# A new order list and another first fill for a planned attention and feed-forward kernel

## The chip, the cores and the metric

The kernel runs on one core of one Trainium2 chip. The metric is the device time of one execution in microseconds (us), the median of several runs. The core has five engines that matter here: TensorE (PE in the profile; its weight loads are PEld), VectorE (DVE), ScalarE (ACT), GpSimd (POOL), and SyncE (SP), which here only issues DMA transfers. Each engine runs its own instructions in their order and waits on semaphores for the others.

## The reference

Inputs `q`, `k`, `v` have 8 batches, 8 heads, 576 positions and a head size of 64, all float32. Attention works in chunks: the 576 positions are 9 chunks of 64, and each chunk looks only at itself.

```python
scores = scale * np.matmul(q_c, k_c.transpose(0, 1, 2, 4, 3))     # per chunk of 64
attn = softmax(scores); out = np.matmul(attn, v_c)
x = out.transpose(0, 2, 1, 3).reshape(B, S, 512)
h = np.maximum(x @ w_in, 0.0)                                      # 512 -> 1024
conv = sum(conv_w[k] * h shifted by k - 1 positions for k in 0, 1, 2)
y = (h * sigmoid(conv)) @ w_out                                    # 1024 -> 512
```

The result is 8 x 576 x 512 in float32. The convolution's neighbours are rows of the same batch; beyond its ends stand zeros.

## The kernel before

**Tiles, units and pairs.** The 4608 rows (batch and position) are cut in three ways. Attention works on 36 tiles of 128 rows (t0 to t35, two chunks each). The first matrix and the convolution work on 12 units of about 384 rows (u0 to u11) times 8 slices of 128 columns of `w_in`, so 96 blocks; a step such as `mm1(1,5)` is unit 1, slice 5. The second matrix works on 18 pairs of tiles (256 rows).

**Precision.** TensorE's fast format is rounded float32 (`float32r`), so each operand is split in a high and a low part (`x_h`, `x_l`, `wi_h`, `wi_l`, `wo_h`, `wo_l`), and each product is three: high times high, high times low, low times high. The `w_in` and `w_out` products therefore take 12 matmuls a block. `w_out` is used with seven products for a pair instead of eight, which need sums and differences of the weights' quarters and of the gated rows (`w_diff`, `f_sum`).

**From load to output.** A tile's q and k are loaded (`load_rows`, in three slots for tiles 0 to 8), transposed on TensorE (`t_pe`, line 198), and copied to SBUF (`t_copy`). `scores` is on TensorE (line 250), the softmax on VectorE and ScalarE (`s_max` to `s_rec`), its division on GpSimd or VectorE (`s_norm`, line 322), its transpose on TensorE again (`p_pe`, line 329), then `attn_v` (line 342). `x_hi` and `x_lo` (line 401) split the result. `mm1` (line 411) multiplies by `w_in`; `h_relu` (line 419 or 421), `c_mid`, `c_left`, `c_right` (line 454), `c_sig` and `c_mul` (line 484) make the gated rows. `f_hi` (lines 77 and 79), `f_lo` (line 502) and `f_sum` (line 505) prepare a pair's factors, `product` (line 515) multiplies by `w_out`, and `o_copy`, `o_both` (line 533) and `o_last` gather the seven products. From tile 9 on, q and k come by way of a copy in device memory and are transposed on VectorE (`t_dve`, line 220), from tile 12 on two tiles share a softmax (`both` on TensorE, `s_fold`, line 306, `s_scale`, line 310, `p_dve`).

**Weights.** They arrive as 64-bit numbers in two w slots, and are turned into float32 by `w_scale` (ScalarE, line 561), `w_shift` (VectorE) and `w_words` (VectorE, line 570), whose end frees the slot. Then come the splits: `w_hi` and `w_left` for `w_in`; for each of four parts of `w_out`: `w_hi_q`, `w_diff` (GpSimd, lines 592 to 594), `w_lo_q` (line 587), `w_hi_d` (line 77) and `w_lo_d` (line 600). All of `w_out` must be ready before the first `product`. Steps 57 to 65 are its last part: 57 the load, 60 `w_words`, 61 `w_hi_q`, 62 `w_diff`, 63 `w_lo_q`, 64 `w_hi_d`, 65 `w_lo_d`.

**What sets the order.** The function doesn't emit instructions as it goes. Each piece of work is a `step()` with an engine, the steps that it must follow, and in `other` the engines that could do it as well; there are 1,873. A list `moved_` gives some steps another engine (an entry is 4 times the step's number plus which of the others). A list `order_` then names all 1,873 steps in the order in which a plan places them: the plan gives out buffers in that order and reckons when each step would begin. Instructions are emitted by that reckoned begin, and at the end each engine's instructions are tied to this order. So a step's neighbours in `order_` on the same engine are what stands ahead of it and behind it in that engine's queue. Where a VectorE step is planned to be running shortly before a GpSimd step, the GpSimd step is made to wait for it ("order at the shared port").

**Fills.** Where the plan sees TensorE idle for over 0.8 us before 110 us, it puts in products of the identity that nothing reads (line 1161 in the profile), so that the engine doesn't stand still. The first fill comes before the first transpose. Each of its entries is two products of 256 columns. `HALVES` says how many entries are made as two products of 256 columns; later entries are one of 512. They read `ident_r`, a copy of `ident` that ScalarE makes.

```python
for _ in range(int((min(gap, 2.9) - 0.3) / 0.43) if pe_free == 2.0 else int((gap - 0.3) / 0.235) if gap > 0.8 else 0):
    n = 2 if filled < HALVES else 4
    for _ in range(4 // n):
        nc.tensor.matmul(banks[idle[-1]][:, 0:P * n], lhsT=ident_r, ...)
```

Of the kernel before, what the change touches and what calls it, by code (L numbers as in the profile page):

```python
# [30 lines left out]
def attn_ffn(ctx: ExitStack, tc: tile.TileContext, q, k, v, w_in, conv_w, w_out, out):  # L31
    nc = tc.nc
# [4 lines left out]
    C = 64  # L37
# [20 lines left out]
    HALVES = 13  # L58
# [32 lines left out]
    banks = [None] * 6  # L91
    ps_y = ExitStack()
    ident = const.tile([P, P], F32, name="ident")
# [865 lines left out]
    for s, over in x_writes:  # L959
# [21 lines left out]
    ]  # L981
    for i, n in (divmod(x, 4) for x in moved_):
# [226 lines left out]
```

## Time and profile before

| what | value |
|---|---|
| median of 3 runs (least, most) | 469.73 us (469.4, 469.97) |
| the profiled execution | 470.28 us, of which its span (first to last instruction) is 468.5 us |
| TensorE busy | 456.2 us, 97% of the span |
| VectorE busy | 409.6 us, 87% |
| GpSimd busy | 283.5 us, 61% |
| ScalarE busy | 263.7 us, 56% |
| chain that ended last, by engine | PE 80%, DVE 9%, DMA 5%, ACT 2% |
| granted TensorE clock | 1.000 over the span |

Busy time is the time in which at least one instruction of the engine runs; the matmuls of TensorE overlap, and their ends are modelled. The chain is followed back from the last instruction to what released it at each step. Idle time of an engine costs something only where another waits for it. The 1.8 us between the span and the profiled execution's own time lie before the first instruction and behind the last.

### The profile page before, as it was taken

How to read it: one execution, taken by the hardware profiler on the slowest of the kernel's cores; microseconds unless marked ns; L12 is line 12 of the kernel's file. 1: busy time of each engine (PE TensorE's matmuls, PEld its weight loads, DVE VectorE, ACT ScalarE, POOL GpSimd, SP SyncE). 2: the span in 40 equal slices, each digit the busy share in tenths (PEclk: the TensorE clock that was granted, in tenths of full speed). 3: DMA queues.
4: the chain of work that ended last, by engine and by line, in shares of the span. 5: the costliest groups of instructions: out<-in, count | busy, mean ns of one | idle time of the engine just before them, and what ended most of it. 6: DMA issues, size and time to landing. Idle time of an engine off the chain costs nothing.

```text
span 468.5 us, 13076 instructions
## 1 busy us (share of the span) xinstructions
PE 456.2 (97%) x5287; PEld 444.3 (95%) x5287; DVE 409.6 (87%) x771; ACT 263.7 (56%) x544; POOL 283.5 (61%) x256
## 2 busy tenths in 40 slices
PE   7899899999999999999999999999999999999996
PEld 7779798999999999999999999999999999999996
DVE  2899999999999899989788889998989987977784
ACT  3589988756646555564444564455556453542641
POOL 0344768847686654979678967755856643448221
PEclk9999999999999999999999999999999999999999
DMA  7999999999896839687987495741215101100012
GB/s 223 248 305 306 246 149 218 158 177 209 147 158 175 191 95 178 126 158 180 181 182 182 109 172 111 169 128 33 58 35 157 25 24 29 40 17 31 22 46 91
DMA packets 184320, 64.32 MB, mean 137 GB/s; under 512 B 155564, under 2 KB 175044, under 8 KB 184260
## 3 DMA queue, kind: packets, MB, share of 16 engines
q1 hardware_dynamic: 184260, 63.48, 62.7%
q8 instruction: 42, 0.69, 0.6%
q14 instruction: 18, 0.15, 0.1%
HBM read 50.88 MB, written 23.59 MB: 159 GB/s over the span
## 4 chain that ended last, share of the span: by engine, by line
PE 80%; DVE 9%; DMA 5%; ACT 2%; issue 1%; SPq 1%; POOL 1%; DVEq 0%; ACTq 0%; POOLq 0%
PE b_ps L411 36%; PE b_ps L515 36%; DVE gt L454 2%; PE sx_ps L250 2%; PE sx_ps L342 2%; PE z_ps L342 2%; DMA v<-in_v 1%; DMA w<-in_moe_w_out 1%; DVE f L502 1%; DMA qk<-in_k 1%; DMA w<-in_moe_conv_w 1%; DVE wt L570 1%; PE z_ps L250 1%; PE b_ps L329 1%; SPq L129 1%
## 5 line engine op out<-in xcount | busy, mean ns | idle before, releaser
L515 PE MATMUL b_ps<-wo_h,f 128*128 128x256 f32 x1008 | 190.9, 282 | 0.4 <-DVE wt L533 0.3
L515 PEld LDWEIGHTS b_ps<-wo_h,f 128*128 128x128 f32 x1008 | 158.8, 188 | 2.0 <-issue 0.5
L515 PE MATMUL b_ps<-wo_l,f 128*128 128x256 f32 x504 | 141.2, 280 | 0.0
L454 DVE SCALAR_TENSOR_TENSOR gt<-b_ps,cw,gt 128x384 f32<-128x384 f32 (+3 forms) x208 | 116.4, 576 | 11.2 <-ACT gt L449 9.1
L502 POOL TENSOR_TENSOR f<-gt,f 128x512 fp32r<-128x512 f32 x67 | 86.4, 1294 | 45.5 <-ACT f L77 16.3
L515 PEld LDWEIGHTS b_ps<-wo_l,f 128*128 128x128 f32 x504 | 94.9, 188 | 0.0
L411 PE MATMUL b_ps<-x_h,wi_h 128*128 128x386 f32 (+2 forms) x384 | 84.6, 342 | 0.0
L411 PE MATMUL b_ps<-x_l,wi_h 128*128 128x386 f32 (+2 forms) x384 | 83.3, 339 | 0.0
L411 PE MATMUL b_ps<-x_h,wi_l 128*128 128x386 f32 (+2 forms) x384 | 83.1, 338 | 0.0
L465 ACT ACTIVATE gt<-gt 128x384 f32<-128x384 f32 (+2 forms) x96 | 49.9, 524 | 54.5 <-DVE gt L454 54.2
L411 PEld LDWEIGHTS b_ps<-x_l,wi_h 128*128 128x128 f32 x384 | 68.8, 188 | 0.0
L411 PEld LDWEIGHTS b_ps<-x_h,wi_l 128*128 128x128 f32 x384 | 68.6, 188 | 0.0
L449 ACT ACTIVATE gt<-b_ps,cw 128x384 f32<-128x384 f32 (+2 forms) x104 | 56.5, 556 | 20.6 <-DVE b_ps L421 18.5
L411 PEld LDWEIGHTS b_ps<-x_h,wi_h 128*128 128x128 f32 x384 | 65.5, 188 | 1.0 <-ACT gt L449 0.2
L505 POOL TENSOR_TENSOR gt<-gt 128x512 f32<-128x512 f32 x41 | 52.8, 1295 | 15.3 <-DVE gb L505 6.0
L484 DVE SCALAR_TENSOR_TENSOR gt<-gt,b_ps 128x192 f32<-128x192 f32 (+2 forms) x120 | 47.2, 410 | 8.8 <-ACT gt L465 8.5
L419 ACT ACTIVATE b_ps<-b_ps 128x386 f32<-128x386 f32 (+2 forms) x79 | 37.6, 479 | 28.2 <-PE b_ps L411 27.0
L79 POOL CAST f<-gt 128x512 fp32r<-128x512 f32 x43 | 26.9, 625 | 21.2 <-PE b_ps L515 18.0
L527 ACT ACTIVATE wt<-b_ps 128x256 f32<-128x256 f32 x54 | 20.6, 381 | 29.8 <-PE b_ps L515 29.7
L77 ACT CAST f<-gt 128x512 fp32r<-128x512 f32 x44 | 26.9, 617 | 14.8 <-PE b_ps L515 8.5
L502 POOL TENSOR_TENSOR f<-gb,f 128x512 fp32r<-128x512 f32 x18 | 23.2, 1294 | 17.9 <-DVE f L502 9.9
L220 DVE STREAM_TRANSPOSE qkT<-qk 128x1024 f32<-128x1024 f32 (+1 forms) x30 | 33.4, 1121 | 0.0
(99 smaller groups left out, 585.6 us busy)
## 6 DMA issues: line engine op xcount, KB each, us to landing
out<-wt SPq DMA_DIRECT2D x36, 256.0 KB, 2.7
qk<-rows SPq DMA_DIRECT2D x24, 320.0 KB, 5.8
rows<-in_q SPq DMA_DIRECT2D x12, 576.0 KB, 8.1
rows<-in_k SPq DMA_DIRECT2D x12, 576.0 KB, 7.8
qk<-rows SPq DMA_DIRECT2D x24, 256.0 KB, 4.6
v<-in_v SPq DMA_DIRECT2D x21, 256.0 KB, 5.0
w<-in_moe_w_out SPq DMA_DIRECT2D x4, 1024.0 KB, 6.5
wt<-wt SPq DMA_DIRECT2D x48, 64.0 KB, 2.0
```

The source lines that it names most:

```text
L77: nc.scalar.copy(out=out, in_=in_)
L79: ENG[eng].tensor_copy(out=out, in_=in_)
L220: nc.vector.transpose(out=to[:, :, i:i + n], in_=of[:, :, o:o + n])
L411: nc.tensor.matmul(h_ps[:, 0:w], lhsT=wt[:, f // 2, kt, P * (f % 2):P * (f % 2) + P], rhs=xt[:, u % NX, kt, 0:w], start=n == 0, stop=n == ...
L419: nc.scalar.activation(out=h, in_=h, func=AF.Relu)
L449: nc.scalar.mul(out=g, in_=h, mul=cw[:, FT + f:FT + f + 1])
L454: nc.vector.scalar_tensor_tensor(out=g, in0=h, scalar=w, in1=g, op0=ALU.mult, op1=ALU.add)
L465: nc.scalar.activation(out=g, in_=g, func=AF.Tanh, scale=0.5)
L484: nc.vector.scalar_tensor_tensor(out=o, in0=g, scalar=1.0, in1=hv, op0=ALU.add, op1=ALU.mult)
L502: ENG[eng].tensor_tensor(out=part(st, 1), in0=quarter(*src), in1=part(st, 0).bitcast(F32), op=ALU.subtract)
L505: ENG[eng].tensor_tensor(out=quarter(*out_), in0=quarter(*a), in1=quarter(*b), op=op)
L515: nc.tensor.matmul(o, lhsT=part(ft, a)[:, j, :], rhs=w[:, i, j, :], start=first and n == 0, stop=n == 3 * FT // 2 - 1, skip_group_check=True)
```

## The change

Three things change.

1. `order_` is another permutation of the same 1,873 steps. The 176 steps of SP, which issue all transfers, keep their order among themselves. Of the 289 steps of TensorE 229 can be kept in their common order, and the rest change places, mostly with a neighbour or two.
2. `moved_` is another list: 204 steps change engine. The largest groups are 21 `o_copy` from ScalarE to VectorE and 12 back, 20 `f_lo` from VectorE to GpSimd and 20 back, `f_hi` among the three engines (63), `h_relu` from VectorE to ScalarE (12) and back (10), and `f_sum` from GpSimd to VectorE (11) and back (7).
3. The first fill opens with `4 * PADS` = 8 float32 products of 64 x 64 that read `ident`, and then has `FILL` = 7 entries, 14 products of 256 columns. `HALVES` falls from 13 to 9.

```diff
-    HALVES = 13
+    HALVES = 9
+    PADS = 2
+    FILL = 7
...
     moved_ = [
-        89, 113, 141, 165, 186, 225, 353, 505, 793, 801, 817, 969, 977, 1045, 1121, 1129, 1197, 1205, 1465,
...
+        69, 89, 138, 186, 225, 325, 345, 381, 457, 465, 793, 805, 813, 969, 1053, 1093, 1121, 1129, 1197, 1205,
...
     order_ = [
-        84, 85, 103, 87, 88, 0, 104, 18, 1, 86, 2, 105, 3, 90, 4, 5, 89, 91, 6, 122, 92, 19, 20, 7, 106, 107, 8,
...
+        0, 84, 85, 230, 103, 86, 18, 1, 2, 87, 4, 104, 106, 89, 88, 105, 122, 90, 3, 5, 6, 91, 19, 20, 7, 21,
...
-            for _ in range(int((min(gap, 2.9) - 0.3) / 0.43) if pe_free == 2.0 else int((gap - 0.3) / 0.235) if gap > 0.8 else 0):
+            for n in range(4 * PADS if pe_free == 2.0 else 0):
+                o, h = C * (n % 2), C * (n // 2 % 2)
+                nc.tensor.matmul(banks[idle[n // 2 % 2 - 2]][o:o + C, 0:C], lhsT=ident[h:h + C, 0:C], rhs=ident[h:h + C, 0:C], start=True, stop=True)
+            for _ in range(FILL if pe_free == 2.0 else int((gap - 0.3) / 0.235) if gap > 0.8 else 0):
                 n = 2 if filled < HALVES else 4
```

Some neighbours in the lists that the prediction speaks of. On TensorE the second half of tile 1's transpose (106) now stands ahead of tile 0's `scores` (90). On GpSimd before: ... `w_diff` 62, `w_lo_q` 63, `s_norm` of tile 7 (442), `w_lo_d` 65; after: 62, 442, 63, 65. On VectorE `w_words` 60 stands ahead of `s_max` and `s_sub` of tile 7 now. `o_both` of pair 3 is step 549, and the product that waits for it is 552.

## Rows read from the trace of the kernel before

**Rows 1.** Windows: us, busy us (instructions) of each engine, granted clock, DMA share, GB/s.

```profile
9.65:35.00 25.35, 22.59 (x488) 19.08 (x481) 22.74 (x49) 17.88 (x34) 9.47 (x11) 1.00 0.98 280
35.00:80.00 45.00, 42.52 (x446) 39.78 (x445) 44.73 (x98) 41.36 (x85) 29.74 (x27) 1.00 1.04 230
80.00:120.00 40.00, 40.00 (x571) 38.63 (x571) 38.59 (x84) 25.55 (x57) 27.86 (x24) 1.00 1.08 188
120.00:150.00 30.00, 30.00 (x319) 29.80 (x319) 29.06 (x52) 18.81 (x41) 21.25 (x18) 1.00 0.84 157
150.00:170.00 20.00, 19.65 (x259) 19.16 (x258) 18.72 (x30) 10.44 (x23) 13.86 (x14) 1.00 0.58 130
180.00:220.00 40.00, 40.00 (x388) 39.80 (x387) 36.63 (x76) 22.97 (x46) 29.93 (x25) 1.00 0.80 152
```

The engines stand in the order PE, PEld, DVE, ACT, POOL.

**Rows 2.** TensorE's waits up to 82 us: line, released by, us in total, times, longest.

```profile
PE b_ps L198 <- DMA qk<-in_k: 0.9, 2, 0.6
```

**Rows 3.** Timeline of the first 6 us: start, duration, engine, line, operation, count, idle before.

```profile
1.01 0.29 POOL masks.py:199 TENSOR_SCALAR_AFFINE_SELECT ident<-ident 128x128 f32<-128x128 f32 x1
...
2.02 0.30 ACT L96 CAST ident_r<-ident 128x128 fp32r<-128x128 f32 x1
...
2.37 2.93 PE L1161 MATMUL b_ps<-ident_r 128*128 128x256 f32 x12 [2.37 <-ACT ident_r L96]
...
5.24 4.07 PE L198 MATMUL b_ps<-ident,qk 128*64 128x128 f32 x48
```

**Rows 4.** Timeline, TensorE's transposes up to 6.8 us and at 22.8 us.

```profile
5.24 1.96 PE L198 MATMUL b_ps<-ident,qk 128*64 128x128 f32 x15
...
22.77 2.05 PE L198 MATMUL b_ps<-ident,qk 128*64 128x128 f32 x32
```

**Rows 5.** Timeline of 61 to 81 us, the steps ahead of the first product.

```profile
61.66 0.86 PE L411 MATMUL b_ps<-x_l,wi_h 128*128 128x388 f32 x4
...
70.42 0.88 DVE L502 TENSOR_TENSOR f<-gt,f 128x512 fp32r<-128x512 f32 x1
...
71.45 1.28 POOL L592 TENSOR_TENSOR wt<-wt 128x512 f32<-128x512 f32 x1 [0.70 <-DVE f L502]
...
74.33 1.99 POOL L587 TENSOR_TENSOR wo_l<-wt,wo_h 128x256 fp32r<-128x256 f32 x2
74.40 1.05 ACT L77 CAST wo_h<-wt 128x1024 fp32r<-128x1024 f32 x1 [0.44 <-POOL wt L594]
...
76.27 1.05 POOL L322 TENSOR_TENSOR wt<-wt,z 128x512 f32<-128x512 f32 x1
...
77.06 0.60 DVE L484 SCALAR_TENSOR_TENSOR gt<-gt,b_ps 128x192 f32<-128x192 f32 x2
...
77.27 2.40 POOL L600 TENSOR_TENSOR wo_l<-wt,wo_h 128x1024 fp32r<-128x1024 f32 x1
...
77.81 0.63 PE L329 MATMUL b_ps<-ident,wt 128*128 128x128 f32 x4 [0.99 <-ACT b_ps L419]
...
80.53 0.28 PE L515 MATMUL b_ps<-wo_h,f 128*128 128x256 f32 x1
```

**Rows 6.** Groups by line on VectorE: count, busy us, mean ns, idle before.

```profile
L220 DVE STREAM_TRANSPOSE qkT<-qk 128x1024 f32<-128x1024 f32 (+1 forms) x30 | 33.4, 1121 | 0.0
...
L502 DVE TENSOR_TENSOR f<-gt,f 128x512 fp32r<-128x512 f32 x29 | 21.2, 732 | 2.9 <-ACT f L77 1.5 <-POOL f L79 1.0
...
L310 DVE TENSOR_TENSOR wt<-wt,z 128x1024 f32<-128x1024 f32 x4 | 4.9, 1217 | 0.2 <-POOL wt L306 0.2
L79 DVE CAST f<-gt 128x512 fp32r<-128x512 f32 x9 | 3.8, 417 | 1.7 <-PE b_ps L515 1.5
...
L306 DVE TENSOR_TENSOR wt<-wt,z 128x1024 f32<-128x1024 f32 x1 | 1.9, 1883 | 0.0
L279 DVE TENSOR_SCALAR z<-z 128x8 f32<-128x8 f32 (+1 forms) x8 | 1.7, 212 | 0.2
```

**Rows 7.** Timeline of TensorE at the first wait behind 80 us.

```profile
166.23 0.35 PE L515 MATMUL b_ps<-wo_h,f 128*128 128x256 f32 x1 [0.35 <-DVE wt L533]
```

219 rows, old and new, of tables (moved_, order_) are left out of this document.

## The prediction

> **What bounds the kernel now.** I read the windows by stage first, then TensorE's waits, the timeline of the first 6 us and of 60 to 81 us, the chain of waits, and last the groups by line for durations. The windows [rows 1] say that the stages have different limits. From 9.65 to 35 us the DMA share is 0.98, and TensorE waits for q and k to land, 0.9 us in two waits [rows 2]. From 35 to 80 us VectorE is busy 44.73 of 45 us. From 80 us on TensorE is: 40.00 of 40, 30.00 of 30, 19.65 of 20, 40.00 of 40. All of its work is fixed, so from 80 us on the end can only move by what its first w_out product moves, plus or minus any new wait. That product starts at 80.53 [rows 5]; 0.35 us is TensorE's one wait between there and 170 us, at 166.23, for `o_both` of pair 3 (line 533) on VectorE [rows 7]. So two gates count: the first product at 80.5, and VectorE's queue at 166.
>
> I numbered the steps in the order in which `step()` is called and read both order lists per engine. What a moved step has ahead of it on its own engine is then a list of names, and each name has a duration.
>
> **The first fill.** Today it waits for `ident_r`, whose cast ends at 2.32; `ident` is there at 1.30 [rows 3]. Eight float32 products need only `ident`, so TensorE starts about 1.0 us earlier. A float32 product stands in the trace as two records, so sixteen; the nearest rows are the transposes' records at 0.13 us each before the pace doubles (1.96 us for 15) and 0.064 after (2.05 us for 32) [rows 4], though twice as wide. Sixteen thus take 1.0 to 2.1 us at most and at their narrower width about half, and fit before 2.37. Then come 14 products instead of 12. Twelve took 2.93 us up to 5.30 [rows 3], so 0.24 each: the first transpose starts 0.3 to 0.5 us later if the pace stays, and up to 1 us of transposes is saved if the pace doubles 1 us or more earlier. Both ends are followed by waits for q and k (0.9 us, [rows 2]) that no faster TensorE shortens, as the DMA share is 0.98 [rows 1] and the loads are asked for in the same order. I take 0 and keep -1.0 and +0.4. The granted clock is given as 1.00 (2.4 GHz) in every window of [rows 1], while the records of [rows 4] double in pace after TensorE had run without a gap since 2.37.
>
> **The tiles at the start.** The second half of tile 1's transpose now stands ahead of tile 0's scores, so these wait for tile 1's k; behind them stands VectorE's `s_max`, whose engine has 2.61 us idle in this stretch [rows 1]. The half costs about 1.0 us (16 records of 0.064, [rows 4]), and it is only exchanged with the scores. Later transposes of tiles 1, 2 and 5 and `p_pe` change places in the same way. Cover: the waits for loads. Without it, at most that 1.0 us either way; I take 0. On SP's queue nothing passes anything else, since its 176 steps keep their order; a load can still be issued later where the step that frees its slot is later. The `w_words` steps, which free the w slots, have between 1.4 us less and 2.5 us more ahead of them on VectorE, the last four +2.5, +0.5, -1.2 and -3.0: no clear direction, 0.
>
> **The last quarter of w_out and the first product.** The first product needs all of `wo_h` and `wo_l`. The last piece is steps 60 to 65: GpSimd's three subtractions of `w_diff` begin at 71.45 after a 0.70 wait, `w_lo_q` takes 1.99, then `s_norm` of tile 7 1.05, then `w_lo_d` 2.40, which ends at 79.67 [rows 5]. TensorE meanwhile stood 0.99 us until the transpose of tile 7 could start at 77.81. Two things were needed for it: that `s_norm`, done at 77.32, and a free PSUM bank, which `c_mul` of block (1,2) gave back at 77.66 (the ScalarE line named in the row ended in the same moment). After the change `s_norm` stands ahead of `w_lo_q` and comes 1.99 us earlier; the second `c_mul` of unit 1 has 0.6 us less ahead of it, but which bank the transpose gets can't be read from the list, so between 0.35 and 0.99 of the wait go. What is late next? `w_lo_d`. GpSimd has 1.4 us less ahead of it (five steps out, among them `w_lo_q` of another quarter, three in), and `w_words` 60 has 3.0 us less ahead on VectorE. From `w_diff` to the end the same four steps take 8.2 us, so a start 0.7 to 3.0 us earlier ends at 76.7 to 79.0. But `w_hi_d` on ScalarE, 74.40 to 75.45 with a 0.44 wait, has 2.3 us more ahead: in the worst case it ends at 77.75 and `w_lo_d` at 80.15, 0.5 us later than now; in the best it loses its wait, ends at 75.0 and `w_lo_d` at 77.4, 2.3 us earlier. Bounds of the first product: -2.3 to +0.5; I take -1.0, the whole wait, which is near their middle. VectorE's `f_lo` for this product has 8.1 us more ahead of it (nine convolution steps of unit 1 now come first): done at 71.3 now [rows 5], at 79.4 then, just in time. One gate lies before: the products of unit 1 with `x_l` start at 61.66 [rows 5] on the heels of `x_lo` of tile 6, which has 0.9 us more ahead. It is hidden if a third of VectorE's 2.61 idle us before 35 us goes.
>
> **VectorE's queue up to 166 us.** 204 steps change engine. At `o_both` of pair 3 the lists differ so, by [rows 6]: `f_lo` and `f_sum`, six in and four out at 0.73, +1.46; `w_left`, one half in, one half and one whole (1.22) out, -1.22; `w_lo_q` in at about the whole tile's 1.22; a `w_hi` and net one `f_hi` in, 2 x 0.42; `p_copy` in, 0.73; `t_dve` in, 1.12; `s_scale` out, -1.22; an `h_relu` in for a `c_mul` out, of nearly one size; two of 0.21 out, -0.42. Sum +2.5 us more on VectorE ahead of the gate. The cover is idle time: 2.61 + 0.27 + 1.41 + 0.94 + 1.28 = 6.5 us up to 170 us [rows 1]. If r of it is filled, the gate moves by 2.5 - r: r of 0 would give +2.5, r of 6.5 would give -4.0, though no further than the first product allows. Beyond 170 VectorE has 3.4 idle us in 40, and I count the moves there (most of the 21 `o_copy` and 10 `h_relu` that go to VectorE, and of the 12 and 12 that go to ScalarE) at 0: TensorE's busy 40.00 of 40 hides them; a wait among them would cost at most some tenths each, like the 0.35.
>
> One row more bears on r. `s_fold` on VectorE took 1.88 us where `s_scale`, the same shape, takes 1.22 [rows 6]: 0.66 us lost while GpSimd ran a subtraction. The Trainium skill (SBUF — State Buffer, section "SBUF: two separate sides") says that VectorE's operations with two SBUF inputs and GpSimd's lock one shared pair of ports against each other for a whole instruction. By that rule six in and four out on VectorE's `f_lo`/`f_sum` cost no more than their 0.73, since each leaves GpSimd; without it, the same. It speaks against the change only where a moved pair falls together: 0.66 each.
>
> **Sum.** First fill 0, tiles 0, first product -1.0, gate at 166: of its 0.35 wait I take 0.1, as the extra 2.5 us leave little. -1.1 us. Against the profiled execution (470.28, of which 468.5 is the span) that is 469.2; the median of the three runs is 469.73, so 468.6.
>
> **The rivals.**
> *A, slower:* VectorE's extra 2.5 us come through at `o_both` of pair 3. For it: 44.73 of 45 busy, and that gate is the one wait that TensorE has there. Against it: 2.61 us idle before 35 us. It decides from r below 1.6 on (2.5 - 1.6 = 0.9 us); at r = 0.7 it is +1.8, 471.5.
> *B, no change:* the first product comes 1 us earlier, and the gate at 166 stays where it was, r of 1.6 to 3.4; the microsecond becomes a longer wait there. 469.7. For it: VectorE is 94% to 97% busy beside a full TensorE from 80 to 170 us [rows 1], so work moved there comes out as a wait.
> *C, much faster:* the pace of TensorE doubles during the first fill, tiles 0 and 1 are through 1.0 us earlier, and this isn't eaten by the waits for loads, so VectorE starts its stage earlier: the forecast's 1.1 and that 1.0, 467.6. Against it: the 0.98 share of DMA [rows 1]. The Trainium skill (TensorE: Matmul & The Clock Gate, "What's actually happening") has the array throttled by default and released by activity; by that rule an earlier start releases earlier, which is this rival, and the doubled pace in [rows 4] agrees with it.
> That the change doesn't do what it says would be a load issued in another order or a start of the fill still at 2.37; then the fill's terms are 0 anyway.
>
> **How the numbers follow.** Forecast 0.42, C 0.06, B 0.28, A 0.24. Less than 0.2% (0.94 us) either way can't be told from no change: faster 0.48, same 0.28, slower 0.24. The range must hold 0.8. Below it reaches to the lower bound of the first product, -2.3, with a little of C: 466.8. Above, to A at r = 0.8, +1.7: 471.4. The likeliest case alone has 467.4 to 468.8.
>
> **What would show it.** Right: the fill's first record at about 1.4; no wait near 1 us before the transpose of tile 7; the first record with `wo_h` at 79 to 80; TensorE then without a wait over 0.4 us up to 180. Wrong: the first product earlier and a wait of 1 us or more at a product or a `both` between 140 and 180, with VectorE named as releaser (B, A); the products of unit 1 with `x_l` later than 62.5 (VectorE's head didn't fill its idle time); tile 2's transposes over a microsecond earlier and VectorE's stage with them (C).

## The result: 1% slower, and the profile after

The changed kernel takes 474.43 us (median of four executions, 473.34 to 476.39); the kernel before, run beside it, 469.85. The ratio is 1.0084, with a 95% interval of 1.0057 to 1.011. In a second comparison (after_again, below) it gave 473.48, 1.0078 (1.0055 to 1.0101). The forecast was 468.6 and its range ended at 471.4.

The profiled execution took 473.34 us, its span is 471.6, against 468.5 before. Here are its windows, in the stretches of [rows 1] (us, busy us and instructions of PE, PEld, DVE, ACT, POOL, then granted clock, DMA share, GB/s):

```profile
9.65:35.00 25.35, 22.44 (x475) 19.17 (x472) 22.72 (x50) 16.70 (x33) 8.10 (x8) 0.93 0.95 276
35.00:80.00 45.00, 43.28 (x463) 40.97 (x462) 44.74 (x98) 42.31 (x86) 28.96 (x24) 1.00 1.03 224
80.00:120.00 40.00, 38.70 (x535) 37.24 (x533) 38.97 (x84) 22.47 (x52) 28.63 (x27) 1.00 1.08 186
120.00:150.00 30.00, 29.74 (x341) 29.29 (x340) 27.90 (x52) 18.05 (x37) 19.01 (x17) 1.00 0.88 168
150.00:170.00 20.00, 20.00 (x258) 19.30 (x257) 19.25 (x32) 10.93 (x23) 15.99 (x14) 1.00 0.58 134
```

From 35 to 80 us TensorE is busier than before (43.28 of 45 us against 42.52). Then, where it was busy without a gap, it is not: 38.70 of 40 and 29.74 of 30. Which waits these are, the timeline of TensorE names (start, duration, engine, line, operation, count, idle before and releaser; lines are two higher than before):

```profile
1.36 0.70 PE L1163 MATMUL b_ps<-ident 64*64 64x64 f32 x16 [1.36 <-POOL ident masks.py:199]
2.38 3.35 PE L1167 MATMUL b_ps<-ident_r 128*128 128x256 f32 x14 [0.31 <-ACT ident_r L98]
...
62.56 0.87 PE L413 MATMUL b_ps<-x_l,wi_h 128*128 128x388 f32 x4
...
77.52 0.60 PE L331 MATMUL b_ps<-ident,wt 128*128 128x128 f32 x4
...
80.07 0.28 PE L517 MATMUL b_ps<-wo_h,f 128*128 128x256 f32 x1
...
84.28 0.69 PE L252 MATMUL sx_ps<-qkT 64*64 64x64 f32 x32 [0.34 <-DVE qkT L222]
...
109.82 0.94 PE L413 MATMUL b_ps<-x_h,wi_h 128*128 128x386 f32 x4 [0.84 <-DVE gb L486]
...
136.74 0.35 PE L517 MATMUL b_ps<-wo_h,f 128*128 128x256 f32 x1 [0.26 <-ACT wt L529]
...
380.47 0.51 PE L517 MATMUL b_ps<-wo_h,f 128*128 128x256 f32 x2 [0.19 <-POOL f L504]
...
408.86 0.94 PE L413 MATMUL b_ps<-x_h,wi_h 128*128 128x388 f32 x4 [0.53 <-ACT gt L451]
```

The reader is to see three things. The fill starts at 1.36 and the 0.99 us wait ahead of the transpose of tile 7 (77.52) is gone, as forecast; the first product starts at 80.07 instead of 80.53 [rows 5]. Behind it stand five waits over 0.15 us of which the kernel before has none, while its own at 166.23 [rows 7] is gone. The last one is put down to ScalarE's `c_mid` (line 451) of another block, which ended at 408.74; VectorE's `c_mul` (10,6), whose PSUM bank TensorE's `mm1(10,5)` takes, ended at 408.71. The idle time counted in a row is only that beyond the modelled end of the matmul before, so a wait costs more than its number.

To see what each wait is worth at the end, I worked out TensorE's **lag** from all its records: each kind of record counts its usual spacing, fillers count nothing, and the lag is how much later the same amount of work is reached than in the profiled execution of before. It is sure only where both orders have done the same work; the times here are at or near such points.

| time in the kernel before, us | 81 | 106 | 157 | 170 | 226 | 328 | 358 | 379 | 414 | 464 |
|---|---|---|---|---|---|---|---|---|---|---|
| changed kernel | -0.5 | 0.1 | 1.9 | 1.5 | 1.7 | 1.7 | 2.0 | 3.0 | 4.1 | 3.8 |

So half a microsecond is won at the first product, 2 us are lost between 81 and 170 us, nothing happens for 160 us, and some 2.4 us are lost between 340 and 414. (Behind the last product 0.7 us come back: the span differs by 3.1.) The five rows hold 2.2 us of idle time, about half of it. The rest stands in no row: the two rows behind 340 us count 0.72, and TensorE's records also start 0.1 to 0.3 us later than their usual spacing at 346.8, 357.9, 370.3, 374.7 and 406.7, where little or no idle time is counted. Two profiled executions of the changed kernel (this one and after_again's) lose 1.9 and 1.8 us from 81 to 170 and 2.5 and 2.1 from 340 to 414, so a difference of some 0.4 us over such a stretch between single executions says nothing.

### The profile page after: what moved, and what is told of

Read it like the earlier page. It is cut to its first block, busy times and chain, and to the rows that moved or that the text cites. A ratio compares the mean times of both kernels' runs of the same rounds, so it can differ in the third digit from the quotient of the medians.

```text
span 471.6 us, 13089 instructions
## 1 busy us (share of the span) xinstructions
PE 459.3 (97%) x5300; PEld 446.6 (95%) x5300; DVE 413.5 (88%) x784; ACT 255.9 (54%) x529; POOL 286.0 (61%) x258
## 4 chain that ended last, share of the span: by engine, by line
PE 71%; DVE 15%; ACT 4%; DMA 4%; issue 2%; SPq 2%; POOL 2%; DVEq 0%; ACTq 0%; POOLq 0%
PE b_ps L517 33%; PE b_ps L413 31%; DVE gt L456 3%; PE sx_ps L344 2%; DVE wt L572 2%; PE sx_ps L252 1%; PE z_ps L252 1%; DMA w<-in_moe_conv_w 1%; PE z_ps L344 1%; ACT gt L451 1%; DMA w<-in_moe_w_in 1%; DMA wt<-wt 1%; DVE gt L486 1%; DVE x_l L403 1%; DVE wt L266 1%
## 5 line engine op out<-in xcount | busy, mean ns | idle before, releaser
L456 DVE SCALAR_TENSOR_TENSOR gt<-b_ps,cw,gt 128x384 f32<-128x384 f32 (+3 forms) x208 | 117.7, 580 | 12.2 <-ACT gt L451 9.3
L504 POOL TENSOR_TENSOR f<-gt,f 128x512 fp32r<-128x512 f32 x70 | 90.8, 1302 | 56.0 <-ACT f L79 20.5
L421 ACT ACTIVATE b_ps<-b_ps 128x386 f32<-128x386 f32 (+2 forms) x81 | 38.8, 479 | 43.9 <-PE b_ps L413 43.6
L81 POOL CAST f<-gt 128x512 fp32r<-128x512 f32 x46 | 28.1, 614 | 23.4 <-PE b_ps L517 10.0
L529 ACT ACTIVATE wt<-b_ps 128x256 f32<-128x256 f32 x45 | 17.1, 380 | 26.6 <-PE b_ps L517 25.7
L308 POOL TENSOR_TENSOR wt<-wt,z 128x1024 f32<-128x1024 f32 x10 | 19.2, 1920 | 18.3 <-DVE z L284 17.0
L79 ACT CAST f<-gt 128x512 fp32r<-128x512 f32 x37 | 22.8, 618 | 9.4 <-PE b_ps L517 5.8
```

What stands on the lines that cost most here:

```text
L79: nc.scalar.copy(out=out, in_=in_)
L81: ENG[eng].tensor_copy(out=out, in_=in_)
L421: nc.scalar.activation(out=h, in_=h, func=AF.Relu)
L456: nc.vector.scalar_tensor_tensor(out=g, in0=h, scalar=w, in1=g, op0=ALU.mult, op1=ALU.add)
L504: ENG[eng].tensor_tensor(out=part(st, 1), in0=quarter(*src), in1=part(st, 0).bitcast(F32), op=ALU.subtract)
```

## The experiments

In the diffs AFTER and BEFORE stand for the two order lists; `moved_` always goes along with the list from which a step's place is taken, unless the diff says otherwise. Lags are those of one profiled execution each.

**Which part of the change, and where.** Four kernels cut the change in pieces.

fill_only, against the kernel before:

```diff
-    HALVES = 13
+    HALVES = 9
+    PADS = 2
+    FILL = 7
```

> The order list and the engines of before, with the new fill alone (eight float32 products, fourteen products of 256 columns, nine entries with halves). Theory Q (queues: in the changed kernel other work stands ahead of what TensorE waits for, on VectorE near 84, 110, 136 and 408 us and on GpSimd near 380 us; the fill has no part in it): the 0.4 us by which the first transpose starts later is eaten by the waits for q and k, so 469.4 to 470.6, within 0.2% of before, and TensorE's only waits after 80 us are the ones near 166 and 454 us. Rival F (the fill): the granted clock, which fell to 0.50 between 20.6 and 24 us in the changed kernel, falls here too, and the wide fillers near 30 us push the stages back: 471 to 474.

order_only, against the changed kernel:

```diff
-    HALVES = 9
-    PADS = 2
-    FILL = 7
+    HALVES = 13
+    PADS = 0
+    FILL = 6
```

> The order list and the engines of after, with the fill of before. Theory Q: 473.3 to 475.5, as the changed kernel, with its waits near 84, 110, 136, 380 and 408 us. Rival F: 469.5 to 471.

head_only, against the changed kernel, and tail_only, against the kernel before:

```diff
-    order_ = AFTER
+    order_ = AFTER[:728] + [i for i in BEFORE if i not in AFTER[:728]]
...
-    order_ = BEFORE
+    order_ = BEFORE[:728] + [i for i in AFTER if i not in BEFORE[:728]]
```

> The changed kernel up to place 728 of its order (near 166 us), with its fill; behind that the order and the engines of before. Theory Q: the waits near 84, 110 and 136 us stay, those near 380 and 408 us go; TensorE's lag on before, 1.7 us from 200 to 315 us in the changed kernel, stays as it is to the end: 471.0 to 472.2. Rival H (all of the loss comes from the head, and the waits of the tail are its echo): 473.5 to 475. Rival F says the same as H.

> The kernel before, with its fill, up to place 728 of its order; behind that the order and the engines of after. Theory Q: the waits near 370, 380 and 408 us come alone, 2.3 us in the changed kernel, less the 0.3 us near 454 us that goes: 471.3 to 472.5. Rivals H and F: 469.4 to 470.6.

| kernel | median, us | ratio to before (95%) | lag at 81 | 157 | 226 | 328 | 414 |
|---|---|---|---|---|---|---|---|
| fill_only | 469.88 | 0.9994 (0.9982 to 1.0005) | -0.9 | -0.9 | -0.5 | -0.4 | -0.4 |
| order_only | 474.66 | 1.0101 (1.0086 to 1.0117) | -0.6 | 2.5 | 2.3 | 2.8 | 4.8 |
| head_only | 471.56 | 1.0036 (1.0024 to 1.0049) | -1.0 | 1.3 | 1.7 | 1.7 | 1.7 |
| tail_only | 472.78 | 1.0066 (1.0049 to 1.0082) | 0.5 | 0.5 | 1.7 | 2.1 | 3.9 |

Theory Q has the times of the first three; F and H fall. The fill costs nothing and gives nothing that can be measured in time. The loss of the head stays nearly as it is to the end (a lag of 1.4 us at 170 us and 1.7 from 226 us on, 1.3 us in time), and the tail makes its own. tail_only is 0.3 us above its range: 1.2 us of its lag arise where the two orders are joined, 0.5 at the gate at 167 us (a wait of 0.89 us for VectorE, 0.35 before) and 0.7 behind it up to 190 us. The wait near 408 us that Q named comes in neither order_only nor tail_only; there a wait stands near 371 us (0.63 and 0.38 us).

**Engines or order.** Two kernels mix the lists.

after_order_before_engines, against the changed kernel; before_order_after_engines, against the kernel before:

```diff
-    moved_ = MOVED_AFTER
+    moved_ = MOVED_BEFORE
...
-    moved_ = MOVED_BEFORE
+    moved_ = MOVED_AFTER
```

> The changed kernel with its order list and its fill, but every step on the engine that it had before. Theory E (which engine a step runs on makes the waits): those near 84, 110, 380 and 408 us go, 469.5 to 471.5. Rival O (the order makes them): 473.5 to 475.5. Rival M (an order fits only the engines that it was made with, and every mix is worse than either): over 476.

> The order list and the fill of before, but every step on the engine that it has in the changed kernel. Theory E: 473 to 475.5. Rival O: 469.5 to 471. Rival M: over 475.5.

514.42 us, 1.0924 (1.0893 to 1.0955), and 526.18 us, 1.119 (1.1159 to 1.1221). Theory M: neither list is better or worse by itself, they are made for each other. TensorE's three largest groups of waits in the first and in the second (line, released by, us in total, times, longest):

```profile
PE b_ps L517 <- POOL f L504: 5.1, 10, 0.8
PE b_ps L517 <- DVE gb L486: 4.1, 3, 3.3
PE b_ps L413 <- DVE gt L486: 3.8, 2, 3.6
```

```profile
PE b_ps L517 <- POOL f L504: 7.8, 9, 3.4
PE b_ps L413 <- DVE gb L486: 4.9, 7, 1.5
PE b_ps L517 <- DVE wt L535: 3.8, 3, 1.5
```

No single wait explains 44 and 56 us. Behind the first product, which comes 1.9 and 5.1 us later than before, TensorE's counted waits add up to 27.0 and 36.3 us, some 30 and 40 of them over 0.1 us. In part the clock comes on top: it was granted at 0.50 for some 14 and 10 us of these two executions (mean 0.986 and 0.989). That a step which comes to an engine at a place chosen for another engine stands in front of work that is due sooner is how I read it; no run takes these waits apart.

**The head: what stood in front.** In the changed kernel the chain of waits at 84 and at 110 us reads (start, duration, engine and line; PE's piece is the one that had waited):

```profile
81.86 0.40 DVE gt L456
82.26 0.72 DVE f L504
82.98 1.16 DVE qkT L222
84.14 0.14 issue
84.28 0.69 PE sx_ps L252 x32
...
107.33 0.68 DVE wt L266
108.01 0.11 DVE z L284
108.12 0.56 DVE f L504
108.68 0.48 DVE b_ps L423
109.16 0.32 DVE gt L486
109.47 0.21 DVE gb L486
109.68 0.14 issue
109.82 2.34 PE b_ps L413 x12
```

VectorE has no gap in either, and in both an `f_lo` (line 504) runs there that was on GpSimd before: step 203 ahead of the transpose of tile 9, step 378 ahead of the `c_mul` of block (2,6) that gives back a bank. A third, step 1603, stands ahead of `c_mul` (10,6) at 407 us. three_flo_back puts these three back:

```diff
     moved_ = [
-        813,
-        1513,
-        6413,
```

> The changed kernel with three f_lo steps (203, 378 and 1603) back on GpSimd, where they were before; 0.7 us less stands on VectorE ahead of the transpose of tile 9, of c_mul(2,6) and of c_mul(10,6), for which TensorE waits near 84, 110 and 408 us. Theory Q: 0.34 of the wait near 84, 0.65 of the 0.84 near 110 and 0.5 near 408 go, at most 1.5 us and at least 1.0: 472.8 to 473.5, or 1.0045 to 1.007 of before. Rival P (GpSimd, which takes 1.3 us for an f_lo, becomes the late one, above all from 85 to 93 us where it has no gap): 474 to 475, with waits for GpSimd's f_lo in their place.

472.83 us, 1.0056 (1.0043 to 1.0069). That is in theory Q's range, but the interval overlaps with the changed kernel's (1.0057 to 1.011, and 1.0055 to 1.0101 in after_again), so the gain has to be read from the rows. Its waits there:

```profile
87.50 0.51 PE L517 MATMUL b_ps<-wo_h,f 128*128 128x256 f32 x2 [0.36 <-POOL f L504]
109.38 0.93 PE L413 MATMUL b_ps<-x_h,wi_h 128*128 128x386 f32 x4 [0.26 <-DVE gb L486]
...
406.25 0.36 PE L517 MATMUL b_ps<-wo_h,f 128*128 128x256 f32 x1 [0.36 <-DVE gb L486]
```

0.84 has become 0.26, the wait at 84.28 is gone, and the one at 408.86 is down to 0.15 (at 408.06). Rival P has its share: GpSimd, which now has the first `f_lo`, is late at 87.5, and a smaller wait for another `c_mul` stands at 406.25. The lag says what each step was worth: from 81 to 97 us it grows by 0.8 (changed kernel 0.6), from 106 to 111 by 0.4 (1.0), from 393 to 412 by 1.0 (1.1). So step 378 gives 0.6 us back, and the other two only exchange one wait for another. The lag behind 226 us falls from 1.7 to 1.15. Of the 1.9 us that the changed kernel's head loses from 81 to 170 us, 1.5 stay, 0.9 of them in pieces of 0.1 to 0.3 us between 111 and 165 us that no run isolates.

**The tail: engines again?** late_engines_back puts 18 steps of 355 to 383 us back on their engines:

```diff
     moved_ = [
-        5794, 5805, 5821, 5829, 5841, 6245, 6269, 6277, 6285, 6289, 6293, 6297,
+        5777, 5786, 5789, 5797, 6133, 6278, 6281,
```

> The changed kernel with the 18 steps that changed engine between places 1515 and 1590 of its order (some 355 to 383 us) back on their engines of before. Theory Q: TensorE's lag on before no longer grows between 340 and 385 us, where it grew by 1.3 us; the wait near 408 us stays: 472.8 to 473.7, or 1.0045 to 1.007 of before. Rival O (the order of these steps, not their engines): 474 to 475.5, with the waits near 370 and 380 us where they were.

473.73 us, 1.0076 (1.0062 to 1.009). Theory Q fails here, though the time lies at the edge of its range: from 328 to 414 us the lag grows by 2.5 us, as in the changed kernel (2.4), and the waits only shift:

```profile
370.03 0.38 PE L517 MATMUL b_ps<-wo_h,f 128*128 128x256 f32 x1 [0.31 <-DVE gt L486]
384.46 0.50 PE L517 MATMUL b_ps<-wo_h,f 128*128 128x256 f32 x2 [0.29 <-POOL f L504]
408.53 0.94 PE L413 MATMUL b_ps<-x_h,wi_h 128*128 128x388 f32 x4 [0.53 <-ACT gt L451]
```

slice_320_385 puts that stretch alone, with its order and its engines, into the kernel before:

```diff
-    order_ = BEFORE
+    order_ = BEFORE[:1327] + AFTER[1327:1592] + [i for i in BEFORE if i not in AFTER[:1592]]
```

> The kernel before with the order and the engines of the changed one in places 1327 to 1592 alone (some 318 to 385 us). Theory Q: TensorE's lag on before grows in that stretch, as it did by 1.7 us in the run with the tail alone, and nowhere else: 471.3 to 472.2, or 1.003 to 1.0045 of before. Rival (the stretch is late only because of what the order did before it): 469.5 to 470.6.

472.68 us, 1.0056 (1.004 to 1.0073). Its lag is 0.2 at 328 us and 1.8 at 379, which is Q's 1.6; another 0.7 comes behind the join at 392, which puts the time above the range. So the stretch is late by itself.

slice_order_alone gives the slice's order to the engines of before, slice_engines_alone its engines to the order of before:

```diff
-    moved_ = MOVED_OF_THE_SLICE
+    moved_ = MOVED_BEFORE
...
-    order_ = BEFORE[:1327] + AFTER[1327:1592] + [i for i in BEFORE if i not in AFTER[:1592]]
+    order_ = BEFORE
```

> The kernel before with the order of the changed one in places 1327 to 1592 (some 318 to 385 us), every step on its engine of before. Both together cost 1.6 us there and 0.7 us at the join. Theory O (the order costs it): lag of 1.3 us or more at 385 us, 471.5 to 473. Theory E (the engines cost it): under 0.5 us, 469.6 to 470.5. Theory M (order and engines fit only each other): 3 us or more, over 473, with waits that the slice with both did not have.

> The kernel before, in its own order, with the 40 steps of places 1327 to 1592 that changed engine on their new engines. Theory E: lag of 1.3 us or more at 385 us, 471.5 to 473. Theory O: under 0.5 us, 469.6 to 470.5. Theory M: 3 us or more, over 473.

477.74 us, 1.0146 (1.012 to 1.0173), and 474.06 us, 1.0064 (1.0041 to 1.0087). Over the slice and its join the lag grows from 3.1 to 9.7 us in the first (its profiled execution was 3.1 us late since its first 35 us, below) and from 0.4 to 4.6 in the second, each by more than both together (0.2 to 2.5). Theory M again; waits of the first, then of the second:

```profile
350.96 0.51 PE L517 MATMUL b_ps<-wo_h,f 128*128 128x256 f32 x2 [0.69 <-POOL f L504]
369.00 0.39 PE L517 MATMUL b_ps<-wo_h,f 128*128 128x256 f32 x1 [0.91 <-DVE gt L486]
375.82 0.38 PE L517 MATMUL b_ps<-wo_h,f 128*128 128x256 f32 x1 [0.66 <-DVE gt L486]
399.80 0.94 PE L413 MATMUL b_ps<-x_h,wi_h 128*128 128x388 f32 x4 [0.79 <-DVE gb L486]
```

```profile
352.29 0.39 PE L517 MATMUL b_ps<-wo_h,f 128*128 128x256 f32 x1 [1.49 <-DVE wt L535]
382.47 0.50 PE L517 MATMUL b_ps<-wo_h,f 128*128 128x256 f32 x2 [0.49 <-POOL f L504]
384.90 0.51 PE L517 MATMUL b_ps<-wo_h,f 128*128 128x256 f32 x2 [0.75 <-POOL f L504]
```

mended takes three_flo_back and puts single steps of the tail where TensorE seemed to need them:

```diff
     # each step is taken out of order_ and put right behind the second one
+    1510 behind 1524, 1656 behind 1717, 1445 behind 1640, 1446 behind 1445, 1447 behind 1571
...
     # engines of before for these steps
+    203, 378, 1603, 1447, 1455
```

> The changed kernel with the three f_lo steps (203, 378, 1603) on GpSimd, and, near 370 and 405 us, the steps put back that stood ahead of TensorE's waits there: p_dve of two pairs behind the c_mul that frees the next bank, o_copy 1455 on ScalarE, f_sum 1445 and f_hi 1446 ahead of the work for later products, f_lo 1447 on VectorE. Theory Q: the waits near 370, 380 and 406 us go, some 1.0 us on top of what the three steps gave: 471.3 to 472.2, or 1.002 to 1.0045 of before. Rival M (what is moved out of one queue's way is late at another): 472.5 to 474, with new waits between 365 and 410 us.

472.85 us, 1.0058 (1.0042 to 1.0074): rival M by the time. The wait at 380 us is gone and there is a new one, for the `o_copy` that went back to ScalarE and is late there:

```profile
375.86 0.36 PE L517 MATMUL b_ps<-wo_h,f 128*128 128x256 f32 x1 [0.86 <-ACT wt L529]
```

From 340 to 414 us its lag grows by 1.8 us (2.5 and 2.1 in the two executions of the changed kernel), so the five moves are worth 0.3 to 0.7 us there. This execution also has a stop of 0.58 us inside a block, at 228.11, for which its row names no releaser; it costs 0.9 us of lag, and none of the moved steps stands near it.

**Is the earlier first product worth anything alone?** to_first_product takes the changed kernel up to about 75 us; to_first_product_old_fill is the same with the fill of before; head_to_95 takes it up to about 95 us, with `f_lo` 203 on GpSimd:

```diff
-    order_ = AFTER
+    order_ = AFTER[:320] + [i for i in BEFORE if i not in AFTER[:320]]    # then 564 right behind 311
...
-    order_ = AFTER
+    order_ = AFTER[:438] + [i for i in BEFORE if i not in AFTER[:438]]    # and 813 out of moved_
```

> The changed kernel with its fill up to place 320 of its order (some 75 us), then the order and the engines of before; the transpose of tile 9 (step 564) is put two convolution steps earlier, since 0.8 us more stands ahead of it. Theory Q: the first product starts 0.5 to 1.0 us earlier than before, no wait near 84 or 110 us, and TensorE keeps that up to the gate at 166 us: 469.0 to 469.9, or 0.9975 to 0.9995 of before. Rival B (VectorE's extra 0.8 us comes out at the gate): 470 to 470.8, with a wait of over 0.8 us there.

> The same with the fill of before. Theory Q, with the order alone as the cause of the earlier first product and nothing from the fill: as with the new fill within 0.3 us, first product 0.5 to 1.0 us earlier. Rival (the fill brings the lead): first product as before, 80.3 to 81, time 469.8 to 470.5.

> The changed kernel with its fill up to place 438 of its order (some 95 us), with f_lo 203 on GpSimd; behind that the order and the engines of before. Theory Q (the earlier first product is a gain wherever no longer queue follows): first product at 79.6 to 80.2 us, some 0.3 us of waits from 84 to 88 us, TensorE 0.3 to 0.7 us ahead of before from 100 us to the end: 469.2 to 469.9, or 0.9985 to 1 of before. Rival B (VectorE is late at one of the waits behind it and takes the lead back): 470 to 471.2.

471.74 us, 1.0032 (1.0015 to 1.0049); 472.05 us, 1.0042 (1.0027 to 1.0058); 470.96 us, 1.0016 (0.9996 to 1.0035). The first two lie above both of their ranges and can't answer the question: at the join a new wait of 1.31 us for VectorE's `c_mul` stands at 76.49 (77.70), more than the one that went, and their first product is later, at 81.71 and 82.92. The third is in rival B's range. Its first product was at 82.42 in the profiled execution, whose first 35 us were slow (below), and from 79 to 105 us its lag grows by 1.7 us, the last 0.9 of it behind the join; so it can't show what the earlier product is worth either. No kernel of this study beats the one before.

**The granted clock near 20 us.** It fell in the changed kernel (0.93 in the first window above). TensorE's three waits ahead of the fall, and finer windows of the changed kernel:

```profile
17.60 0.46 PE L252 MATMUL sx_ps<-qkT 64*64 64x64 f32 x16 [0.90 <-ACT qkT L79]
18.92 0.66 PE L331 MATMUL b_ps<-ident,wt 128*128 128x128 f32 x4 [0.86 <-DVE wt L324]
20.41 0.79 PE L331 MATMUL b_ps<-ident,wt 128*128 128x128 f32 x4 [0.67 <-POOL wt L324]
```

```profile
18.00:20.00 2.00, 0.88 (x10) 0.55 (x5) 1.86 (x7) 1.94 (x4) 0.68 (x1) 1.00 0.86 196
20.00:22.00 2.00, 1.59 (x36) 1.29 (x40) 1.97 (x4) 1.53 (x4) 0.36 (x1) 0.70 0.92 247
22.00:24.00 2.00, 2.00 (x54) 1.88 (x48) 1.44 (x5) 1.17 (x3) 0.31 (x1) 0.50 1.06 313
24.00:26.00 2.00, 2.00 (x30) 1.79 (x26) 1.97 (x4) 1.30 (x3) 0.73 (x1) 0.95 0.93 318
```

TensorE had been busy 0.88 of 2 us from 18 to 20, between waits of 0.90, 0.86 and 0.67; then it ran at 0.50 (1.2 GHz) for some 3.4 us, by the means of the next three rows. The kernel before has a fill of six products at 18.55 there, which the new plan doesn't make. Two kernels add seven products to the last two of these waits:

```diff
+            for _ in range({117: 4, 98: 3}.get(i, 0) if idle else 0):
+                nc.tensor.matmul(banks[idle[-1]][:, 0:2 * P], lhsT=ident_r, ...)
             pe_free = begin[i] + steps[i]["cost"]
```

> head_to_95 with seven more filler products of 256 columns, four ahead of p_pe of tile 1 and three ahead of p_pe of tile 0, where TensorE waited 0.87 and 0.67 us near 19 and 21 us. Theory K (these waits let the granted clock fall, and that costs time): mean clock 0.997 or more in nearly all runs, median down by 0.3 to 1.0 us against head_to_95, or 0.998 to 1.001 of before. Rival W (the fall comes from the longer wait of 1.4 us at the scores of tile 2, which the fillers don't cover, or costs nothing): clock as low as in head_to_95, 1.000 to 1.0035 of before.

> The changed kernel with the same seven fillers. Theory K: mean clock 0.997 or more, 0.2 to 0.8 us less than the changed kernel. Rival W: as the changed kernel within 0.2 us, or the fall as before.

> The changed kernel again, to be compared with the one with the seven fillers: 1.0075 to 1.010 of before, mean clock under 0.997 in half of its runs or more.

The mean clock was 0.992 to 0.996 in 8 of 12 executions of head_to_95 and in 4 of 6 of after_again; with the seven products it was 0.998 or more in all 18. So these waits let it fall. What it costs is less clear. after_fillers took 472.91 us, 1.0058 (1.0042 to 1.0075), beside 473.48, 1.0078 (1.0055 to 1.0101), for after_again on the same chip; that is K's direction, 0.6 us, but the intervals overlap. head_to_95_fillers took 471.10, 1.0031 (1.0016 to 1.0047), no less than head_to_95. Within after_again the two executions at 0.999 took 472.2 and 472.6, the four below 473.1 to 475.3; but head_to_95_fillers, at 0.998 or more throughout, spreads as far, from 470.3 to 473.6. What makes the first stage late may lower the clock as well, so which is the cause isn't shown. The fall is not the cause of the kernel's loss: order_only at a mean clock of 1.000 took 474.38.

## Why the prediction was wrong

**Right: the first fill at 0.** It begins at 1.36 as forecast, the first transpose comes 0.4 us later (5.66), and q and k come no sooner. fill_only is within 0.2% of before. (In its one profile the first product came at 79.62, so a part of the next term may be the fill's; order_only, with the fill of before, had it at 79.95 all the same.)

**Right in place, about right in size, and in part by luck: the first product, -1.0.** `s_norm` of tile 7 now ends at 74.8 and the transpose doesn't wait. In the eight profiled executions with the new order and no early join the first product starts at 79.2 to 80.4; with the order of before and its fill at 80.5 to 81.0 in four and at 83.6 in a fifth. In the pair of the forecast it is 0.46, because the products of unit 1 with `x_l` begin at 62.56 instead of 61.66 [rows 5]. I had written that the 0.9 us more ahead of `x_lo` of tile 6 are hidden if a third of VectorE's idle time before 35 us goes; it did not go (2.61 us before, 2.63 after).

The bounds, -2.3 to +0.5, came from `w_lo_d` (step 65) as the next thing to be late, and that was wrong. The first product does not need all of `w_out`, as the kernel's description and the prediction say: `w_lo_d` writes parts 3 to 6 of `wo_l`, and the first product reads part 0. In the changed kernel the step waits and ends at 80.46, later than before (79.67) and than the worst case (80.15), while the first product starts at 80.07:

```profile
78.04 2.42 POOL L602 TENSOR_TENSOR wo_l<-wt,wo_h 128x1024 fp32r<-128x1024 f32 x1 [1.29 <-ACT gt L451]
```

In all eight of those executions the first product starts 0.4 us before this step ends. TensorE has no wait over 0.1 us from 61.78 to 84.28, so what set its start was TensorE's own earlier waits. That -1.0 was near the middle of these bounds counts for nothing.

**Wrong: the gates that I counted between 80 and 170 us.** The step that failed is "So two gates count". The sum for the second, +2.5 less r, was fair: `o_both` of pair 3 ends 1.07 us later, so r was 1.4, below the 1.6 from which rival A decides (as far as the two can be told apart: TensorE itself was over 1 us late by then). But TensorE never waits there, as it has lost some 2 us before, part of them at three gates that the prediction left out because TensorE had no wait at them. For the transpose of tile 9 the same reckoning by lists gives some 0.9 us more ahead on VectorE, and it starts 0.90 us later (82.90, before 82.00); the scores of tile 9 had 1.06 us to spare before and wait 0.34 now. For the `mm1` of block (2,7) the order of TensorE changed too: a product now stands ahead of it, and it takes the bank that `c_mul` (2,6) frees, where it took one that a `p_copy` on ScalarE had freed; that `c_mul` ends 1.05 us later than before. The third is an `o_copy`, at 136.74. three_flo_back shows for the second of the three that the step on VectorE made the wait (0.84 with it, 0.26 without); for the first it only exchanged the wait, and the third was not tested. Some 0.9 us of the head's loss, this third wait among them, lie in pieces of 0.1 to 0.3 us whose cause stays open.

**Wrong: everything behind 170 us at 0**, since "TensorE's busy 40.00 of 40 hides them", with some tenths for a wait. It cost some 2.4 us of lag. A full TensorE says that nothing was late, not how much later it may come. The trace of before says that: of TensorE's 230 steps behind 80 us, 60 begin within 0.5 us of the end of the last thing that they need from another engine (a result or a buffer given back), and 106 within 1 us. Moving a step of 0.4 to 1.3 us ahead of any of them can make a wait. In the changed kernel `f_sum` 1445 stands further back in VectorE's queue and ends at 377.3 (before 371.7), `f_lo` 1447 follows on GpSimd up to 380.4 (before, on VectorE, 376.0), and the product that needs it waits. What is shown is that this stretch is late by itself and that neither its order nor its engines alone is to blame; which single step would mend it stays open, since late_engines_back and mended for the most part exchanged one wait for another.

**Rivals.** A was nearest: slower, through VectorE's queue behind the first product, with 0.24, but at other places, and it priced only the head. B's longer wait at 166 did not come, and C had no part in it. The price for a pair that falls together on VectorE and GpSimd holds in the one step that can be compared, the same `s_fold`: it took 1.88 us before, with GpSimd's `f_lo` beside it for its first 0.79 us, and takes 1.55 now, with 0.47: 0.33 us less for 0.32 us less of overlap.

**A term that was missing:** the waits at 17 to 20 us and the clock that falls behind them; 0.6 us in one pair of kernels, inside the noise, and nothing in the other.

## What to carry to other kernels

Where a list fixes the order of every engine, an engine that is busy without a gap can have next to no cover (here a quarter of TensorE's steps had less than 0.5 us): for a change of that list, work out for every step of the bound engine what it needs last and how long before, and compare the lists at each of them that has less to spare than the steps moved ahead of it. A new order and a new choice of engines have to be judged together; either alone was 9% and 12% slower here. A change made in several places can be cut at places where both lists have done nearly the same steps (at place 728 they differ by two), and the pieces then show where the loss arises: 1.3 us for the head and 2.5 for the tail, against 4.4 for the order as a whole (order_only). They don't simply add up, since 1.2 us of the tail's lag was made at and behind the join.

## What was not expected

Between executions the first 35 us differ more than the rest. In the two profiles of the changed kernel the first product starts at 80.07 and 79.19, and from there to TensorE's last record it is 387.6 and 387.4 us. From the first product to TensorE's last record the four kernels with the order of before behind 80 us take 383.4 to 384.0 us, but that product itself starts anywhere from 79.6 to 82.9 (83.6 in slice_order_alone, where the DMA share falls to 0.14 from 30 to 32 us). A difference in the first stage should therefore be read from several profiled executions.

The clock fell in an execution-dependent way: of two profiles with the same first stage, three_flo_back's has a mean of 0.57 from 20 to 24 us, behind waits of 0.53, 0.87 and 0.67 us, and late_engines_back's has 1.00 there, behind waits of 0.63, 0.86 and 0.67. The Trainium skill (TensorE: Matmul & The Clock Gate, section "What's actually happening") has two levels and the array throttled unless it is busy, and says that the moment at which it switches depends on the execution; the 0.50 and 1.00 of the windows and this spread agree with it.
